# Attention and gated MLP on one core: batches 0 and 1 read q and k as six tokens per partition with both heads side by side, the strided scores of the other batches take 36 rows, and the three lists of steps are written anew

## The chip, the cores and the metric

The kernel runs on one core of a Trainium2 chip. A core has five engines that run side by side and each take their own instructions in order: TensorE (PE; its weight loads are shown apart as PEld), VectorE (DVE), ScalarE (ACT), GpSimd (POOL) and SyncE (SP), which here only issues transfers. Sixteen DMA engines move data between HBM and the core's memory, SBUF; TensorE writes to PSUM, which this kernel uses as four slots of two banks. The metric is device time in microseconds (us); lower is better.

## The reference, cut to what matters

Eight batches, eight heads, 576 positions, head size 64, all float32. Heads 0 to 3 have a local mask (a window of 32), heads 4 to 7 a strided mask (every 32nd position). The attention's output is the input of a gated MLP that mixes positions with a 576x576 matrix.

```python
scores = scale * np.matmul(q, k.transpose(0, 1, 3, 2))
mask_local = (rel >= 0) & (rel < stride)
mask_strided = (rel >= 0) & (pos[None, :] % stride == pos[:, None] % stride)
masks = np.stack([mask_local if h < H // 2 else mask_strided for h in range(H)], axis=0)
scores = np.where(masks[None, :, :, :], scores, -1000000000.0)
...
attn = attn / (np.sum(attn, axis=-1, keepdims=True) + 1e-09)
return np.matmul(attn, v).astype(np.float32)
...
h = x @ w_in                      # then gelu, split in u and v
v_n = (v - mu) / np.sqrt(var + 1e-06) * g_ln
v_s = np.einsum('ts,bsd->btd', w_sg, v_n) + b_sg[None, :, None]
gated = u * v_s
return (x + gated @ w_out).astype(np.float32)
```

## The kernel before, in words

Two heads share the 128 partitions: a pair is called hh (0 and 1 local, 2 and 3 strided). Per batch, the attention of four pairs gives x, and the MLP runs on it in four stages of matmuls: `v` and `u` (x times the two halves of w_in), `sg` (the mixing of positions) and `o` (w_out). Float32 factors are split in a high and a low part of a type that TensorE takes in one pass, so each product is three matmuls (names ending in h and l: `wih`, `wil`, `wsh`, `wsl`, `woh`, `wol`; `xt`, `vg` hold both parts). In the first batch's stretch all weights are loaded and split too, by ACT, DVE and POOL.

Nothing is scheduled by a program while the kernel is built: each engine gets its instructions in the order in which the steps stand in three lists of words. `START` is run once (batch 0's attention, the weights, batch 0's MLP beside batch 1's attention), `CYCLE` for batches 1 to 6 (the MLP of batch b, the attention of b + 1, loads for b + 2), `LAST` for batch 7. In a word like `SB^:0` the letters name the step (the table `STEPS`), the number is its pair or chunk, `@2` the PSUM slots it takes, `^` that the step's other engine does it (DVE in place of POOL, ACT in place of DVE, DVE in place of ACT or POOL in place of DVE, by the step). A sign behind the letters says which batch is meant: `-` the current one, none the next one for capital letters, `+` the one after; `=` marks steps of the weights.

The steps of this change: `LR` (`row_load`), `RQ` and `RK` (`row_turn`), `CQ` and `CK` (`row_copy`) bring q and k of batches 0 and 1 to SBUF and turn them so that the head's 64 numbers lie along the partitions. Before, a partition gets nine tokens of one head, 2304 bytes in one piece, and a turn is 18 plain float32 matmuls of 64x64 against the identity, which TensorE runs in two passes (36 records). Batches 2 to 7 take another way: `LQ` (`qk_load`) and `TQ` (`qk_transpose`, on DVE), which is kept. `SS` (`strided_scores`) makes 32 small matmuls per pair, `MK` (`sm_mask`) adds the mask on DVE, `MX`, `SB`, `EX`, `SU`, `ML` are the other steps of the softmax, `PS` and `PL` turn the weights of attention on TensorE, `PV`, `PW`, `VA` multiply them with v. `XH`, `XL`, `XR`, `XD` split x, transpose it and store it to HBM (from the ACT queue) for the residual.

Profile rows name the outputs: `tqq`, `tqk` (turns), `sa`, `sr` (local scores), `ss` (strided scores), `ptl`, `pts` (turned weights of attention), `ol`, `os` (their products with v). In the order's rows a name carries a running number.

Of the kernel before, what the change touches and what calls it, by code (L numbers as in the profile page):

```python
# [31 lines left out]
ch=:3 SB-:3 VY-@0:0 CL-:4 VX-:0 cd=:9 MX-:2 XH-:1 EX-:3 SB-:2 ch=:0 cc=:4 cl=:13 XR-:0 XHa-:0
XL-:1 RQ@3:1 RK@2:1 XHb-:0 cg=:9 XR-:1 EX-:2 LV-:2 ca=:6 SU-:2 CK:1 XLb-:0 RK@3:0 TZ:0 SU-:3 cb=:6
ch=:9 ML-:2 CQ:1 ML-^:3 XD-:0 XD-:1 PS-@1:2 RQ@2:0 LV-:3 CS-:2 cb=:2 PS-@0:3 cb=:8 CK:0 XLa-:0
cc=:6 CS-:3 cc=:2 wb= PV-@1:2 CQ^:0 PW-:2 cd=:4 cc=:8 XH-:2 wc= cl=:5 SL@2:0 cd=:6 PV-@3:3 cd=:2
wl=:0 SL@0:1 wd= cl=:7 XL-:2 cg=:2 we= LR:2 cg=:4 ch=:2 ca=:13 LZ:0 lg= PW-:3 XR-:2 MK:0 va@1:0
cd=^:8 ch=^:4 XH-:3 vb:0 ca=:5 wl=:4 cb=:5 XD-:2 cb=:13 ca=:7 wt=@2:0 vc:0 cl=:11 LR:3 XL-:3 cc=:5
wh=:0 cg=:8 vd:0 RQ@0:2 xt RK@2:2 g:0 cb=:7 CQ:2 MX:0 v@1:2 va@0:1 vb:1 CK:2 ca=:11 wm=:0 wo=
cd=^:5 cc=:7 wl=:2 cg=:6 ls:0 vc:1 lm:0 ch=:8 cd=:7 vh vl LV:0 cb=:11 SB^:0 cc=:11 cg=:5 cl=:10
wp= cg=:7 LQ+:0 lr:0 wt=@2:4 ch=:5 cc=:13 vd:1 LZ:1 EX:0 ch=:7 ch=^:6 XR-:3 g:1 SU:0 cd=^:13  # L40
RK@3:3 RQ@1:3 CK:3 cg=:13 CQ^:3 u@3:2 SS@1:2 u@0:1 wh=:4 cd=:11 lh:0 LV:1 g:2 wt=@1:2 u@3:0 ca=:10
ls:1 TZ+:0 ug:2 cl=:15 ll:0 MK:2 ug:1 cb=:10 XD-:3 SS@2:3 u@3:3 wh=:2 lm:1 ls:2 cg=:11 lr:1 wm=:4
ML:0 cc=:10 wl=:3 lr:2 ch=:11 ug:0 lm:2 lh:1 wt=@1:3 ca=:15 ug:3 lh:2 MX:2 MK:3 wm=:2 cb=:15
cd=:10 wh=:3 MX:3 ll:1 ll:2 wm=:3 cl=:14 TQ+:0 SB:3 cc=:15 SB:2 EX:2 cg=:10 TZ+:1 LQ+:1 cd=^:15
SU:2 PL@23:0 cl=:12 s@0:0 CL:0 s@1:1 sm:0 CM:0 VA@3:1 EX:3 ML:2 TQ+:1 sh:0 PS@1:2 VA@2:0 sm:1
ca=:12 s@0:2 XR:1 cb=:12 cg=:15 cc=:12 ch=:15 ch=:10 sh:1 ch=:13 s@1:3 SU:3 LQ+:3 CS:2 ca=:14 XH:1
sl^:0 sm:2 XL:1 XH:0 sl^:1 XD:1 cd=^:12 LV:2 LV:3 o@3:2 XL:0 cg=:12 cb=:14 ML:3 PV@2:2 XR:0 rt
cc=:14 sh:2 XD:0 sm:3 ch=:12 PW:2 PS@1:3 sl^:2 o@0:0 cd=^:14 sh:3 LZ+:1 o:1 XH:2 CS:3 r sl:3 o:3
PV@1:3 PW:3 XR:2 cg=:14 ch=^:14 LV+:1 o2:0 XR:3 LQ+:2 XH:3 XD:3 XL:2 o2:1 LZ+:0 os:1 o2:3 os:0
# [7 lines left out]
CM^:0 sh:2 SU:2 sm:3 sl^:2 o@0:0 VA@2:1 TQ+:0 sh:3 LV:2 VA@1:0 o@3:4 o:1 sl^:3 EX:3 XH:0 XH:1 ML:2
SU:3 o2:1 XR:0 LV:3 XL:0 o2:4 os:1 o@1:2 o2:0 os:4 TQ+:1 od:1 os:0 o2:2 ML^:3 LZ+:0 os:2 PS@0:2
od:4 PS@3:3 XR:1 XD:0 od:0 XL:1 o:3 CS:3 o2:3 CS:2 XD:1 PV@2:3 LQ+:2 od:2 PV@3:2 PW:3 PW:2 XH:2
os:3 LZ+:1 XH:3 XR:2 XL:3 XR:3 LV+:1 XD:3 XL:2 XD:2 od:3 LV+:0  # L60
# [980 lines left out]
```

## Time and profile before

| | us |
|---|---|
| median of three runs | 577.9 (572.86 to 579.85) |
| the profiled execution, its own time | 579.74 |
| its span, first to last instruction | 577.9 |
| PE busy in the span | 550.6 (95%) |
| DVE busy in the span | 377.2 (65%) |
| ACT, POOL busy in the span | 205.7 (36%), 187.7 (32%) |

The page of the profile tells how long each engine was busy, then cuts the span into 40 slices of 14.4 us with the busy share of each in tenths. The views of the trace used below are stretches of time (busy us of each engine, DMA share and rate), waits (what ended an engine's idle time), the timeline of one engine (instructions of one form merged, with the idle time ahead of them in brackets) and groups of instructions by form (busy us, mean ns of one). Where instructions overlap, as matmuls do, the time that one costs is the distance from its start to the next one's, not its length.

### The profile page before, as it was taken

How to read it: one execution, taken by the hardware profiler on the slowest of the kernel's cores; microseconds unless marked ns; L12 is line 12 of the kernel's file. 1: busy time of each engine (PE TensorE's matmuls, PEld its weight loads, DVE VectorE, ACT ScalarE, POOL GpSimd, SP SyncE). 2: the span in 40 equal slices, each digit the busy share in tenths (PEclk: the TensorE clock that was granted, in tenths of full speed). 3: DMA queues.
4: the chain of work that ended last, by engine and by line, in shares of the span. 5: the costliest groups of instructions: out<-in, count | busy, mean ns of one | idle time of the engine just before them, and what ended most of it. 6: DMA issues, size and time to landing. Idle time of an engine off the chain costs nothing.

```text
span 577.9 us, 17955 instructions
## 1 busy us (share of the span) xinstructions
PE 550.6 (95%) x7699; PEld 494.6 (86%) x7699; DVE 377.2 (65%) x685; ACT 205.7 (36%) x330; POOL 187.7 (32%) x407
## 2 busy tenths in 40 slices
PE   6777998999999899999999999999999999999997
...
GB/s 303 238 171 195 113 154 117 165 203 164 38 1 164 158 197 29 11 185 168 163 1 84 199 205 59 2 179 196 151 1 89 195 180 1 1 140 140 2 1 91
DMA packets 244593, 70.13 MB, mean 121 GB/s; under 512 B 228193, under 2 KB 228193, under 8 KB 244514
## 3 DMA queue, kind: packets, MB, share of 16 engines
...
q8 instruction: 60, 0.98, 0.7%
...
## 4 chain that ended last, share of the span: by engine, by line
PE 85%; DMA 7%; DVE 4%; issue 2%; ACT 1%; SPq 1%; ACTq 0%; DVEq 0%
PE sg L82 21%; PE v L82 19%; PE u L82 17%; PE o L82 14%; DMA out_dram<-ob 3%; PE ss L82 3%; PE ol L82 3%; PE os L82 3%; PE sa L82 2%; DMA xd<-xs 1%; DMA stage<-in_moe_w_in_dram 1%; PE ptl L82 1%; DVE ob L82 1%; PE tqq L82 1%; PE pts L82 1%
## 5 line engine op out<-in xcount | busy, mean ns | idle before, releaser
L82 PE MATMUL sg<-wsh,vg 128*128 128x288 f32 x512 | 114.1, 298 | 0.0
L82 PE MATMUL u<-xt,wih 128*128 128x288 f32 x512 | 103.2, 297 | 1.0 <-ACT u L82 1.0
L82 PE MATMUL o<-woh,vg 128*128 128x512 f32 x288 | 94.1, 396 | 2.2 <-DVE ob L82 2.2
L82 PE MATMUL v<-wih,xt 128*128 128x512 f32 x256 | 85.5, 405 | 2.1 <-DVE xs L82 2.1
L82 PEld LDWEIGHTS sg<-wsh,vg 128*128 128x128 f32 x512 | 86.6, 190 | 0.0
L82 PEld LDWEIGHTS u<-xt,wih 128*128 128x128 f32 x512 | 82.2, 188 | 2.1 <-ACT u L82 1.2
L82 PE MATMUL sg<-wsl,vg 128*128 128x288 f32 x256 | 76.1, 297 | 0.1
L82 PE MATMUL u<-xt,wil 128*128 128x288 f32 x256 | 75.5, 295 | 0.0
L82 PEld LDWEIGHTS o<-woh,vg 128*128 128x128 f32 x288 | 54.1, 188 | 13.9 <-DVE ob L82 2.8
L82 DVE TENSOR_TENSOR gt<-sg,u 128x576 f32<-128x576 f32 x32 | 24.2, 757 | 56.6 <-PE sg L82 35.7
L82 PEld LDWEIGHTS v<-wih,xt 128*128 128x128 f32 x256 | 49.1, 192 | 11.4
L82 PE MATMUL o<-wol,vg 128*128 128x512 f32 x144 | 56.3, 391 | 0.0
L82 POOL TENSOR_TENSOR vg<-gt,vg 128x576 fp32r<-128x576 f32 (+2 forms) x45 | 44.8, 1016 | 34.8 <-ACT vg L82 34.8
L82 PE MATMUL v<-wil,xt 128*128 128x512 f32 x128 | 50.9, 398 | 0.0
L82 PEld LDWEIGHTS sg<-wsl,vg 128*128 128x128 f32 x256 | 48.8, 191 | 0.3 <-DVE wsl L82 0.3
L82 DVE TENSOR_TENSOR ob<-o,xn 128x512 f32<-128x512 f32 x32 | 22.0, 691 | 41.3 <-PE o L82 32.8
L82 PEld LDWEIGHTS u<-xt,wil 128*128 128x128 f32 x256 | 48.1, 188 | 0.0
L82 ACT ACT_TABLE_LOAD x18 | 23.1, 1283 | 59.5 <-DMA xd<-xs 58.6
L82 ACT CAST vg<-gt 128x576 fp32r<-128x576 f32 (+2 forms) x48 | 23.1, 514 | 58.1 <-DVE gt L82 53.8
L82 DVE BATCH_NORM_STATS2 bnst<-hv 128x6 f32<-128x512 f32 (+1 forms) x40 | 27.1, 677 | 24.2 <-ACT hv L82 23.9
L82 ACT ACTIVATE u<-u 128x576 f32<-128x576 f32 x32 | 20.0, 649 | 57.0 <-PE u L82 56.5
L82 POOL TENSOR_TENSOR sml<-sml,sr 128x1152 f32<-128x1152 f32 (+2 forms) x9 | 17.2, 1906 | 68.6 <-DVE sr L82 62.7
...
## 6 DMA issues: line engine op xcount, KB each, us to landing
xd<-xs ACTq DMA_DIRECT2D x128, 72.0 KB
...
```

Source lines behind the costliest of these rows:

```text
L82: ins = self.tc.keep_in_program_order(op(*args, **kwargs))
```

## The change

Four edits in the code, and new lists.

A partition now gets six tokens with both heads side by side, so 96 partitions hold a pair. A head's part of a partition is six pieces of 64 numbers, 256 bytes each, and each tensor of a pair is loaded by two DMAs in place of one. The turn is six transposes of 96x128 in place of 18 matmuls of 64x64; the copy from PSUM rearranges accordingly.

For batches 2 to 7 the strided scores take 36 columns of q in place of 64, so that the mask is added in two pieces of 36 partitions, as it was for batches 0 and 1 before, and the memset behind q's last column goes away. A helper tile of `v_tail_copy` is half as long.

```diff
-    ROWS = S // 9
+    ROWS = S // 6
...
         if b == 0:
-            both = p1.tile([P, 2, 9 * D], F32, tag=HOMES[hh], name=f"rows_{b}_{hh}")
+            both = p1.tile([P, 2, 6, P], F32, tag=HOMES[hh], name=f"rows_{b}_{hh}")
...
-            sp.dma_start(
-                raw, src[b, 2 * hh : 2 * hh + 2].rearrange("h (p j) d -> (h p) (j d)", j=9)
+            for hp in range(2):
+                sp.dma_start(
+                    raw[:, :, D * hp : D * hp + D],
+                    src[b, 2 * hh + hp].rearrange("(p j) d -> p j d", j=6),
+                )
...
+        for j in range(6):
+            pe.transpose(
+                ps[:, j // 3, j % 3 * ROWS : j % 3 * ROWS + ROWS], raw[:, j], ident[0:ROWS, 0:ROWS]
             )
...
-        for j in range(9):
-            for hp in range(2):
-                r = slice(ROWS * hp, ROWS * hp + ROWS)
-                pe.matmul(
-                    ps[64 * hp : 64 * hp + 64, j * ROWS : j * ROWS + ROWS],
-                    raw[r, j * D : j * D + D], ident[r, r],
-                    start=True, stop=True,
-                )
...
-                if nm == "q":
-                    pool.memset(tt[:, S : S + ST], 0.0)
...
-                            rows, qc, kc = 64, slice(c * TP, c * TP + 64), slice(c * TP, c * TP + TP)
+                            qc = slice(c * TP, c * TP + TP)
...
-            for r in (slice(0, TP), slice(64, 100)) if b < 2 else (slice(0, 100),):
-                n = r.stop - r.start
+            for r in (slice(0, TP), slice(64, 64 + TP)):
...
-LR-:0 LR-:1 RQ-@2:0 cl=:3 mk= TZ-:0 TZ-:1 RK-@3:0 CQ-^:0 ml= mp=@2 cl=:1 cl=:0 ca=:3 cb=:3 LR-:3
+LR-:0 cl=:3 cl=:1 TZ-:0 RQ-@2:0 LR-:1 RK-@3:0 mk= ca=:1 ca=:3 mp=@1 cl=:0 CK-:0 cb=:1 cb=:3
...
-ug:0 rt lh:1 ll:0 lr:2 u@3:2 ll:1 lh:2 ll:2 MK:3 SB:2 ug:2 SB^:0 s@1:1 sm:1 MX:3 ug:3 EX:2 s@0:0
+lm:2 MK:2 lh:2 ll:0 EX:0 MK:3 ll:1 u@2:3 MX:2 ll:2 SU:0 u@1:0 TZ+:1 s@0:1 TZ+:0 sm:1 TQ+:1 SB^:2
```

What the lists move is seen where the instructions stand. SP's first transfers before: `rows` are q and k of batch 0, `stage` a part of w_in, `cs` of w_out, `wsg` of the mixing matrix, `v` the values.

```order
L82 DMA rows_0_92<-in_q_dram 128x576
L82 DMA rows_0_92<-in_k_dram 128x576
L82 DMA rows_1_95<-in_q_dram 128x576
L82 DMA rows_1_95<-in_k_dram 128x576
L82 DMA stage<-in_moe_w_in_dram 128x1024 x3
L82 DMA rows_3_192<-in_q_dram 128x576
L82 DMA rows_3_192<-in_k_dram 128x576
```

And now, from the same place on, as far as the values of the first two pairs:

```order
L82 DMA rows_0_92<-in_q_dram 96x6x64 x2
L82 DMA rows_0_92<-in_k_dram 96x6x64 x2
L82 DMA stage<-in_moe_w_in_dram 128x1024 x2
L82 DMA rows_1_108<-in_q_dram 96x6x64 x2
L82 DMA rows_1_108<-in_k_dram 96x6x64 x2
L82 DMA stage<-in_moe_w_in_dram 128x1024
L82 DMA rows_3_165<-in_q_dram 96x6x64 x2
L82 DMA rows_3_165<-in_k_dram 96x6x64 x2
L82 DMA rows_2_209<-in_q_dram 96x6x64 x2
L82 DMA rows_2_209<-in_k_dram 96x6x64 x2
```

The loads of the rows have moved little against each other; each is now two DMAs of short pieces. The values of pair 0 come ahead of those of pair 1, and batch 1's first rows (`rowsq_1`, `rowsk_1`) stand between the two.

TensorE in the same stretch, the turns of batch 1 and the first products with the values, before:

```order
L82 MATMUL ol_1_568<-ptl_5_563,v_1_398 64x32 x36
L82 MATMUL ol_0_616<-ptl_5_563,v_0_396 64x32 x4
L82 MATMUL ol_0_616<-ptl_4_621,v_0_396 64x32 x32
L82 MATMUL tqq_1_669<-ident,rowsq_1_504 64x64 x18
L82 MATMUL tqk_1_688<-ident,rowsk_1_506 64x64 x18
L82 MATMUL tqk_0_724<-ident,rowsk_0_612 64x64 x18
L82 MATMUL pts_2_765<-ident,sms_89 128x100 x8
```

and now:

```order
L82 MATMUL ol_0_495<-ptl_5_482,v_0_248 64x32 x4
L82 MATMUL ol_0_495<-ptl_4_493,v_0_248 64x32 x32
L82 MATMUL tqk_1_538<-ident,rowsk_1_397 128x96 x6
L82 MATMUL ol_1_567<-ptl_5_482,v_1_252 64x32 x36
L82 MATMUL pts_2_623<-ident,sms_89 128x100 x8
L82 MATMUL tqq_0_635<-ident,rowsq_0_476 128x96 x6
L82 MATMUL tqq_1_649<-ident,rowsq_1_394 128x96 x6
```

Turns have gone from 18 rows to 6 each, and a turn of batch 1 now stands between the products of pair 0 and pair 1.

ACT in one round of `CYCLE` (batch 2), between the last parts of the normalised v (`t`) and the first gated product (`gt`), before; `sml` and `sms` are the exponentials of the local and the strided scores, and ACT_TABLE_LOAD changes between the tables of gelu and of the exponential:

```order
L82 ACTIVATE t_85<-hv_2_3210,y_2_3383 64x512
L82 ACTIVATE u_2_3431<-u_2_3399 128x576
L82 ACTIVATE u_3_3467<-u_3_3296 128x576
L82 ACT_TABLE_LOAD
L82 ACTIVATE sms_89<-sms_89 100x16x36
L82 ACTIVATE sml_3108<-sml_3108 128x1152
L82 CAST vg<-gt_1_3463 128x576
```

and now:

```order
L82 ACTIVATE t_85<-hv_2_2977,y_2_3181 64x512
L82 ACT_TABLE_LOAD
L82 ACTIVATE sml_2932<-sml_2932 128x1152
L82 ACT_TABLE_LOAD
L82 ACTIVATE u_3_3307<-u_3_3211 128x576
L82 ACTIVATE u_0_3309<-u_0_3243 128x576
L82 CAST vg<-gt_1_3301 128x576
L82 ACT_TABLE_LOAD
L82 ACTIVATE sms_89<-sms_89 100x16x36
```

The local exponential has moved ahead of the last two gelus, so that each round has four table loads in place of two; the whole program has 30 in place of 18. In `CYCLE` TensorE's stages keep their order (v, u, sg, o); the two strided scores stand together in the middle of u (before: one inside v, one after the first quarter of u), and v's first half stands ahead of the local scores.

## Rows read from the trace of the kernel before

**Rows 1.** The page: busy time and share of PE and DVE, and PE's busy tenths in 40 slices.

```profile
PE 550.6 (95%) x7699; PEld 494.6 (86%) x7699; DVE 377.2 (65%) x685; ACT 205.7 (36%) x330; POOL 187.7 (32%) x407
...
PE   6777998999999899999999999999999999999997
```

**Rows 2.** Stretches of the span: from:to, length, then busy us (and instructions) of PE, PEld, DVE, ACT, POOL, the granted share of PE's clock, the DMA share, GB/s. The first is what stands ahead of the first v matmul, the second the rest of batch 0's way to sg, the last a round of CYCLE.

```profile
0.00:50.00 50.00, 33.59 (x1152) 30.74 (x1152) 35.66 (x69) 23.73 (x43) 19.14 (x45) 0.96 0.86 245
50.00:90.00 40.00, 38.96 (x467) 34.42 (x462) 32.63 (x60) 25.07 (x43) 26.67 (x54) 0.96 0.64 131
...
125.00:195.00 70.00, 67.65 (x969) 60.46 (x968) 45.90 (x82) 21.91 (x35) 19.50 (x47) 1.00 0.52 109
```

**Rows 3.** Who PE waited for, us in total, times, longest; the first 95 us.

```profile
PE tqq L82 <- issue: 4.7, 2, 2.9
PE tqq L82 <- DMA rows<-in_q_dram: 4.0, 1, 4.0
PE sr L82 <- issue: 2.9, 1, 2.9
PE sg L82 <- DVE t L82: 1.5, 1, 1.5
...
PE u L82 <- ACT u L82: 1.0, 1, 1.0
```

**Rows 4.** The same from 95 us to the end of the span, the two largest (a third, of 0.2 us, is left).

```profile
PE o L82 <- DVE ob L82: 2.2, 3, 1.2
PE v L82 <- DVE xs L82: 2.1, 1, 2.1
```

**Rows 5.** PE's timeline: start, length, instructions merged, and in brackets the idle time ahead with what ended it. The first two turns, the three stalls that end in "issue", the first v matmuls, two turns between v matmuls, and the first chunk of u with what follows it.

```profile
3.99 2.19 PE L82 MATMUL tqq<-ident,rows 64*64 64x64 f32 x36 [3.99 <-DMA rows<-in_q_dram]
5.94 2.16 PE L82 MATMUL tqk<-ident,rows 64*64 64x64 f32 x36
...
20.61 0.62 PE L82 MATMUL tqq<-ident,rows 64*64 64x64 f32 x13 [2.92 <-issue]
...
33.67 0.97 PE L82 MATMUL tqq<-ident,rowsq 64*64 64x64 f32 x26 [1.82 <-issue]
...
42.37 1.14 PE L82 MATMUL os<-pts,v 36*64 36x36 f32 x64 [1.22 <-ACT pts L82]
...
48.95 0.42 PE L82 MATMUL sr<-kT,qT 64*32 64x64 f32 x10 [2.89 <-issue]
...
50.10 0.79 PE L82 MATMUL v<-wih,xt 128*128 128x512 f32 x1
...
57.70 1.26 PE L82 MATMUL tqq<-ident,rowsq 64*64 64x64 f32 x36
58.80 1.22 PE L82 MATMUL tqk<-ident,rowsk 64*64 64x64 f32 x36
...
70.34 0.54 PE L82 MATMUL u<-xt,wih 128*128 128x288 f32 x2
...
73.72 1.30 PE L82 MATMUL ss<-kT,qT 64*36 64x36 f32 x64
```

**Rows 6.** PE's timeline: eight transposes of 100x128 in the first stretch and what follows them, and sixteen in a round of CYCLE and what follows.

```profile
38.21 0.91 PE L82 MATMUL pts<-ident,sms 100*128 100x100 f32 x8
39.05 1.26 PE L82 MATMUL tqq<-ident,rowsq 64*64 64x64 f32 x36
...
185.46 1.56 PE L82 MATMUL pts<-ident,sms 100*128 100x100 f32 x16 [0.22 <-DVE ob L82]
186.80 0.47 PE L82 MATMUL o<-woh,vg 128*128 128x512 f32 x1
```

**Rows 7.** The page's list of DMA queues: PE's instructions come in the queue named q8 (kind: packets, MB, share of 16 engines).

```profile
q8 instruction: 60, 0.98, 0.7%
```

**Rows 8.** Stretches with the columns of rows 2. From 2 to 6 us the rows of 2304 bytes are on their way; from 20 to 24 mostly pieces of 256 bytes of the values; from 30 to 42 the last transfers ahead of the first v matmul.

```profile
2.00:6.00 4.00, 2.01 (x38) 2.04 (x40) 0.00 (x0) 0.20 (x1) 3.46 (x18) 1.00 0.96 305
...
20.00:22.00 2.00, 1.35 (x22) 1.02 (x22) 1.80 (x5) 0.73 (x2) 0.00 (x0) 1.00 0.94 129
22.00:24.00 2.00, 2.00 (x81) 2.00 (x83) 1.35 (x4) 1.96 (x6) 1.05 (x1) 0.57 1.11 187
...
30.00:36.00 6.00, 3.92 (x172) 3.64 (x164) 5.54 (x12) 3.60 (x8) 3.73 (x5) 1.00 0.56 190
36.00:42.00 6.00, 4.13 (x88) 3.69 (x88) 5.93 (x13) 1.28 (x3) 1.52 (x2) 1.00 0.74 139
```

**Rows 9.** SP's timeline: the issue of the values of pairs 0 and 1 (pieces of 256 bytes) and of pairs 2 and 3.

```profile
13.74 10.61 SPq L82 DMA_DIRECT2D v<-in_v_dram  x8
...
31.68 6.81 SPq L82 DMA_DIRECT2D v<-in_v_dram  x4
```

**Rows 10.** Groups by form, whole span: busy us, mean ns of one. Strided scores with 64 and with 36 columns of q on PE, the mask on DVE in one piece and in two, the table loads of ACT.

```profile
L82 PE MATMUL ss<-kT,qT 64*64 64x36 f32 x768 | 13.7, 224 | 0.0
L82 PE MATMUL ss<-kT,qT 64*36 64x36 f32 x256 | 5.3, 248 | 0.1
L82 DVE TENSOR_TENSOR sms<-ss,mask_s 100x576 f32<-100x576 f32 x12 | 9.0, 748 | 0.2
L82 DVE TENSOR_TENSOR sms<-ss,mask_s 36x576 f32<-36x576 f32 x8 | 6.0, 754 | 3.0 <-PE ss L82 3.0
L82 ACT ACT_TABLE_LOAD x18 | 23.1, 1283 | 59.5 <-DMA xd<-xs 58.6 <-PEq L1023 0.7
```

More of the change, by code (lines that the diff above doesn't have):

```diff
@@ L32 @@
[L32 to L49, printed above, removed]
@@ new lines @@
+SS-@1:2 LV-:1 wh=:1 MK-:2 ca=:4 PL-@30:5 wm=:1 TZ:0 LR:0 CL-:5 cc=:9 SB-:3 PL-@1:4 MX-:2 CL-:4
+VY-@2:0 SB-:2 cd=^:9 CM-:5 cg=:0 VX-:0 cg=:9 RK@3:1 cc=:2 ch=^:9 EX-:3 XR-:0 cb=:4 ca=:8 cb=:8
+TZ:1 EX-:2 SU-:2 CK:1 SU-:3 cc=:8 VA-@0:1 cc=:4 cl=:6 ML-:2 XD-:0 XH-:1 XHa-:0 ML-:3 XR-:1 LV-:2
+LV-:3 PS-@1:2 cl=:5 CS-:2 RQ@3:0 XHb-:0 cd=:8 XL-:1 ca=:6 wb= RQ@1:1 PS-@0:3 PV-@1:2 XLb-:0 wc=
+cb=:6 cl=:13 CQ:0 XD-:1 CS-:3 LR:2 LZ:1 CQ^:1 PW-:2 RK@2:0 PV-@3:3 ch=^:0 XLa-:0 XH-:2 cd=:2 cc=:6
+CK:0 XL-:2 PW-:3 wl=:0 cd=^:4 cl=:7 wd= cg=:8 XH-:3 we= SL@2:0 SL@0:1 va@1:0 XR-:2 vb:0 cg=:4
@@ new lines @@
+cg=:2 XL-:3 ch=:2 ca=:13 wt=@2:0 ca=:5 vc:0 xt wo= XD-:2 vd:0 RQ@2:2 MK:0 ch=^:4 RK@0:2 wh=:0
+cb=:5 g:0 cb=:13 wp= MX:0 cd=:6 CQ:2 v@1:2 va@2:1 cl=:11 lg= LR:3 wm=:0 vb:1 LV:1 cc=:5 wl=:4
+RQ@0:3 ca=:11 ca=:7 LQ+:1 cd=^:5 cg=:6 cg=:5 vh CK:2 ls:0 vc:1 cb=:11 cb=:7 LZ:0 cc=:11 vd:1
+RK@3:3 cc=:13 cc=:7 SB^:0 EX:0 XR-:3 wl=:2 cd=^:7 lr:0 cl=:15 g:1 SS@1:2 vl cg=:7 CQ^:3 ch=^:5
+wt=@0:4 SU:0 g:2 ch=^:7 XD-:3 lm:0 cd=:13 cl=:10 ls:1 cd=^:11 ch=:6 MK:2 CK:3 u@2:1 lm:1 wl=:3
+wh=:4 u@3:2 ML:0 lh:0 wt=@1:2 lr:1 LV:0 ls:2 ug:1 ug:2 SS@2:3 wh=:2 u@3:3 lh:1 LQ+:0 cl=:12 ug:3
@@ new lines @@
+lm:2 LV:3 wt=@2:3 MK:3 u@0:0 lr:2 ll:0 ca=:10 ca=:15 cg=:13 wm=:4 MX:2 wh=:3 lh:2 LQ+:3 ll:1 wm=:2
+wm=:3 ch=:8 TZ+:1 PL@12:0 ll:2 CL:0 cb=:15 cl=:14 cb=:10 cc=:15 ug:0 SB^:2 MX:3 CM:0 s@3:0 TQ+:1
+SB^:3 cd=^:15 cg=:11 cc=:10 sm:0 EX:2 cd=^:10 cg=:10 cg=:15 sh:0 SU:2 EX:3 ch=:13 s@0:1 ca=:12
+sm:1 VA@3:1 XH:1 ML:2 TZ+:0 VA@2:0 TQ+:0 SU:3 PS@1:2 CS:2 XR:1 ML^:3 ch=^:11 XH:0 XD:1 sh:1 sl^:0
+ch=:10 ca=:14 s@0:2 PS@1:3 XL:1 cb=:12 LV:2 s@3:3 rt cc=:12 sl^:1 sm:2 CS^:3 sm:3 o@0:0 sh:2
+cd=:12 r sl^:2 XR:0 cb=:14 XL:0 o@3:2 ch=^:15 o:1 PV@2:3 sh:3 cc=:14 PV@1:2 sl^:3 cg=:12 LZ+:0
@@ L57 @@
[L57 to L60, printed above, removed]
+LQ+:0 v1@0:0 SL@2:0 SL@1:1 v2:0 g:0 MK:0 xt v@2:2 v1@1:1 v2:1 TQ:2 MX:0 vh ls:0 u@2:1 SB:0 g:1 vl
+u@0:2 lr:0 SS@1:2 g:2 lm:0 ug:1 ls:1 lh:0 r lm:1 ug:2 rt lr:1 TQ:3 SS@3:3 ls:2 LQ+:1 lr:2 lh:1
@@ new lines @@
+lm:2 MK:2 lh:2 ll:0 EX:0 MK:3 ll:1 u@2:3 MX:2 ll:2 SU:0 u@1:0 TZ+:1 s@0:1 TZ+:0 sm:1 TQ+:1 SB^:2
+ug:3 ug:0 s@3:0 ML:0 PL@20:0 MX:3 sm:0 sh:1 EX:2 sh:0 SB:3 SU:2 sl^:1 s@1:2 s@3:3 sm:2 TQ+:0 LV:3
+sh:2 CL:0 CM^:0 sm:3 sh:3 VA@0:0 sl:3 sl^:0 VA@3:1 EX:3 o@1:0 XH:0 sl^:2 o:1 o@2:4 XH:1 SU:3 o2:1
+LQ+:2 ML^:3 XR:0 XL:0 o2:4 os:1 o@0:2 o2:0 o2:2 od:1 XL:1 os:4 ML:2 os:0 od:4 LV:2 XD:0 LZ+:0
+PS@1:3 XR:1 od:0 PS@3:2 os:2 CS:2 o:3 o2:3 CS^:3 LZ+:1 PV@1:2 PV@2:3 PW:2 os:3 XD:1 LQ+:3 PW:3
+LV+:1 XH:3 od:3 XH:2 XR:3 od:2 XL:3 XD:3 XL:2 XR:2 XD:2 LV+:0
@@ L67 @@
+s@3:0 s@2:2 sm:0 sh:1 sh:0 sm:3 sm:2 sl^:1 sh:3 sl:3 sh:2 sl^:0 o@0:2 o:3 sl:2 o2:3 o@1:0 os:3
+od:3 o2:2 o2:0 os:2 o@2:4 os:0 o2:4 od:2 os:4 od:0 od:4 o:1 o2:1 os:1 od:1
 """
```

47 lines of the change are left out of this document (20 added, 27 removed).

## The prediction, made before the changed kernel was run

> **What bounds the kernel now.** I read the page first: PE is busy 95% of the span, DVE 65%, and the slices show where PE is not: in the first five, and almost nowhere else [rows 1]. The stretches say it in numbers: PE is idle for 16.4 of the first 50 us, for 1.0 of the next 40, and for 2.4 of a round of CYCLE [rows 2]. So there are two kernels here. From about 50 us on PE sets the pace, and only shorter PE work or a removed wait counts. Ahead of that PE waits, and the question is for what. The list of waits answers in part [rows 3]: 4.0 us for the first rows, which nothing can hide, 7.6 us in three stalls that end in "issue", that is for nothing the profile shows, and 1.0 to 1.5 us here and there for DVE or ACT. Behind 95 us all PE waits together are 4.5 us [rows 4]; that is the most that new lists can win in CYCLE and LAST.
>
> I take the three stalls for late instructions. They stand at 20.6, 33.7 and 48.9 us [rows 5], where PE runs many tiny matmuls. PE's 15,398 instructions (7,699 matmuls and as many weight loads) [rows 1] come in 60 packets of 16 KB [rows 7], so some 257 each, and a turn alone is 72 of them. The stalls come in the stretch whose DMA share is 0.56 to 1.11 [rows 8], so a packet can be late there. The Trainium skill (Runtime: NRT & Kernel Launch, Instruction fetch mechanics) says that engines fetch blocks of 256 instructions ahead and that this is mostly hidden. The packet count agrees; the hiding doesn't, if my reading is right, and by the page's rule the stalls would have another cause and could stay, which is 7.6 us less to win in the fast rival below.
>
> **The turns.** A turn between v matmuls takes 1.10 us at the full clock (57.70 to 58.80), and the first one, at the low level, 1.95 [rows 5]. The new one is six transposes of 96x128. The nearest rows are those of 100x128: eight take 0.84 us, sixteen take 1.34 [rows 6], so 84 to 105 ns each and 0.50 to 0.63 us per turn. No row shows one at the low clock; twice that, 1.0 to 1.26, is the bound. I take 0.55 and a saving of 0.55. Twelve of the sixteen turns stand ahead of the first v matmul (6.6 us of PE work), four behind it (2.2 us). They also take 16 x 60 = 960 instructions out of PE's stream, which is 3.7 of 60 packets, most of them where the stalls are. PE therefore could reach v 6.6 + 7.6 = 14 us earlier, if its operands were there.
>
> **The loads speak against it.** A pair's q and k are 2 x 294,912 bytes. In pieces of 2304 bytes such rows came at 305 GB/s (2 to 6 us, DMA share 0.96): 1.9 us. In pieces of 256 bytes, from 20 to 24 us, the values came at 129 to 187 GB/s with a DMA share of 0.94 to 1.11 [rows 8]: 3.2 to 4.6 us per pair. So each pair costs 1.2 to 2.7 us more of all sixteen engines, and six pairs are needed ahead of v: 7 to 16 us. The Trainium skill (DMA: Bandwidth & Descriptors, Why small descriptors are slow) gives 3 cycles of overhead to the 8 of a 256-byte descriptor; by that alone, as an estimate, a pair would cost about a third more, 0.6 us, and six 4 us. The trace shows more, and I go by its rows.
>
> Is there room? Until 24 us the DMA share is about 1, so there is none; from 30 to 42 us it is 0.56 and 0.74 [rows 8], which leaves 6 x 0.44 + 6 x 0.26 = 4.2 us. The last loads needed ahead of v are the values of pairs 2 and 3, issued from 31.68 to 38.5 [rows 9] and used at 42.37 and after; PE then waits for ACT, not for them [rows 5]. They would come 7 - 4 = 3 to 16 - 4 = 12 us later. I put their landing before at about 40 to 41 (two to three us behind the last issue, an estimate), so 43 to 53 now, and behind it are one product with the values and the local scores of batch 1, which PE does in about 3.5 us. First v matmul: 47 to 56, against 50.1 now. DVE does 35.7 us of work in these 50 [rows 2], of which the new lists change little, so from its first work on it could not let v start before about 41 to 42 either. Within 47 to 56 I take 49.5, nearer to the low end, because PE work no longer adds to it and the values of pair 0 now come ahead of pair 1's: a gain of 0.6 us. That is the core of the forecast: the turns get shorter, and the time goes to the transfers.
>
> **Behind the first v matmul.** Four turns save 2.2 us of PE work that is on the path, since PE was idle for only 1.0 of 40 us there [rows 2]. The waits for `u` (1.0) and `t` (1.5) [rows 3] stay or go with DVE and ACT; DVE has 32.6 us of work in 40 [rows 2], so it has room. I take 1.0 of 2.5.
>
> **Edits that I cost at nothing.** Strided scores of 36 columns: the same number of matmuls. The 64-column form takes 13.7/12 = 1.14 us per pair, the 36-column one 5.3/4 = 1.32 [rows 10], but the latter has strided columns of q, which the new one has not. Bounds 0 to +2.2 us (12 x 0.18); I take 0. The mask: two pieces of 754 ns for one of 748 [rows 10], 12 x 0.76 = 9.1 us more on DVE, 1.5 per round; DVE is busy 45.9 of 70 us there [rows 2]. Queued behind it are the low parts of the normalised v, which sg waits for; without cover it would cost the 1.5 us per round, 9 us in all. Two chunks of u stand between the strided scores and sg, 2 x 3.4 = 6.8 us (70.34 to 73.72 is one) [rows 5]; in that time DVE has two masks of 1.5, two low parts of two operations each and two short steps, some 6 to 7 us: just covered. The twelve more table loads: 12 x 1.283 = 15.4 us of ACT [rows 10], 2.6 per round; ACT is busy 21.9 of 70 us. They delay the last two gelus of u, which are next needed when the second of four sg products is done; ACT has 48 us free per round to catch up. Memsets taken off POOL hide in its idle time.
>
> **CYCLE and LAST.** PE's stages keep their order, and it waits 4.5 us in all [rows 4]. New lists could take these waits away or set up new ones. I count 1.5 us gained, with bounds from -4.5 to +6 (one us more in each of six rounds).
>
> **The sum.** -0.6 (ahead of v) - 2.2 - 1.0 (behind) - 1.5 (rounds) = -5.3 us. The profiled execution's own time is 579.7, so 574.4; that execution stands 1.8 us above the median of 577.9, and against the median it is 572.6, say 573.
>
> **The rivals.**
>
> *The transfers don't bind (fast).* If short pieces cost the low end (7 us) and the room takes 4.2 of them, PE reaches v when DVE allows, at about 42 to 43, 7.5 us earlier. With 3.2 behind and 2 in the rounds that is 577.9 - 12.7 = 565. For it: most of the loads were early before, PE's only long wait for rows is the 4.0 us at the start [rows 3]. Against it: the DMA share near 1 until 24 us, and the stalls may have another cause.
>
> *The transfers bind hard (slower).* At 129 GB/s the loads come 12 us late, the first v matmul moves to 55.5, and PE, idle by stretches, starts it at the low level, where a turn took 1.95 us in place of 1.10 [rows 5]; I allow 1 us for that. +5.4 + 1 - 2.2 = +4, 582. It is slower than before from the point where six pairs cost over some 12 us more, that is at a rate below about 150 GB/s.
>
> *A wait in each round (slower or same).* If DVE's second mask isn't covered, the low parts come 1 to 1.5 us late in six rounds: 573 + 6 to 9 + 1.5 = 580 to 583. DVE has 24 us free per round [rows 2], but the stretch does not tell where.
>
> *The change doesn't do what it says.* Transposes at the low clock as dear as the matmuls were, and the stalls stay: no term of the turns, loads late by 3 us: 578.
>
> **Chances.** Forecast 0.47, fast 0.23, hard 0.15, a wait in each round 0.10, no effect 0.05. Faster by over 2% is below 566.3: most of the fast case and a little of the forecast, 0.20. Slower by over 2% is above 589.5: only where the hard case and the wait in each round come together or are worse than their rows, 0.08. Same: 0.72 (2% is about what a measurement of this kernel can tell from no change). Range: from 562, the fast case with three more us in the rounds, to 585, the hard case and its error; the forecast's own is 568 to 578.
>
> **What would show it.** Turns: six transposes in 0.5 to 0.65 us between v matmuls; more would break that term. Stalls: PE waits ending in "issue" ahead of v should fall from 7.6 us to under 3, and 56 or 57 packets in PE's instruction queue. Loads: PE waits named by rows or values should appear in the first 45 us, with a DMA share near 1 up to about 40 us; if there are none, the fast rival holds. The first v matmul at 47 to 52. Rounds: PE busy at least 68 of 70 us and no DVE wait ahead of sg; if DVE waits of over 1 us stand there in each round, the third rival holds. A first v matmul before 44, or rounds that change by over 1 us each, would make the forecast wrong.

## The result, and the profile after

| | before | after |
|---|---|---|
| median of 20 runs, us | 577.7 (571.5 to 583.0) | 583.8 (578.0 to 590.3) |
| profiled execution: own time, span, us | 579.7, 577.9 | 581.3, 579.2 |
| first v matmul starts at, us | 50.1 | 55.1 |
| last `os` of batch 1 ends at, us | 119.8 | 118.4 |
| from there to the last matmul, us | 454.4 | 457.2 |

The change made the kernel slower: ratio 1.0107, 95% interval 1.0073 to 1.0142. 573 was forecast; the time lies inside the range, on the other side of no change. Ratios here and below leave out runs in the chip's slower state, which the medians keep, so a ratio and its medians can differ by some 0.3%. The profiled execution of after lies 2.5 us under its median and that of before 2.0 above, so the pair shows 1.6 of the 6.1 us. Another profile of after is among the experiments.

The page of after, for [rows 1] and [rows 7]; the fourth line is PE's granted clock in slices:

```profile
PE 543.1 (94%) x7219; PEld 486.7 (84%) x7219; DVE 395.2 (68%) x641; ACT 219.7 (38%) x337; POOL 205.1 (35%) x456
...
PE   3769999999999899999999999999999999999997
...
PEclk9965999999999999999999999999999999999999
...
q8 instruction: 56, 0.92, 0.7%
```

PE has 7.5 us less work and the kernel takes longer. DVE, POOL and ACT have 18, 17 and 14 us more. Stretches of after, for [rows 2] and [rows 8] (columns as there):

```profile
0.00:50.00 50.00, 32.21 (x628) 28.17 (x628) 31.29 (x59) 22.63 (x42) 19.07 (x45) 0.84 1.03 215
50.00:90.00 40.00, 37.57 (x492) 32.88 (x489) 35.41 (x60) 25.41 (x46) 21.52 (x46) 0.91 0.88 168
125.00:195.00 70.00, 69.53 (x1025) 62.27 (x1027) 49.66 (x74) 24.92 (x37) 23.59 (x58) 1.00 0.57 120
...
36.00:42.00 6.00, 3.84 (x80) 3.52 (x80) 5.22 (x11) 1.72 (x3) 2.36 (x2) 0.50 1.05 220
```

The DMA share is 1.03 over the first 50 us (0.86 before), and from 36 to 42 us PE stands at the low level, 1.2 GHz (granted 0.50; the trace has it there from 33.7 to 57.6). The waits of PE up to 95 us, for [rows 3]:

```profile
PE tqq L82 <- DMA rows<-in_q_dram: 9.0, 2, 4.8
PE ol L82 <- DMA v<-in_v_dram: 2.2, 2, 1.7
PE tqk L82 <- DMA rows<-in_k_dram: 1.7, 2, 1.1
PE tqk L82 <- DMA rowsk<-in_k_dram: 1.4, 1, 1.4
```

And from 95 us on, for [rows 4]:

```profile
PE sg L82 <- DVE t L82: 3.9, 5, 1.0
PE u L82 <- DVE hv L82: 1.9, 3, 1.0
PE ptl L82 <- POOL sml L82: 1.8, 5, 0.4
PE ol L82 <- issue: 1.6, 2, 0.9
PE v L82 <- issue: 1.6, 1, 1.6
```

Ahead of v the "issue" stalls are gone (7.6 us to 1.2) and waits for rows and values stand in their place. From 95 us on the waits have grown from 4.5 us to 12.1. PE's timeline of two turns between v matmuls, for [rows 5]:

```profile
62.39 0.66 PE L82 MATMUL tqq<-ident,rowsq 96*128 96x96 f32 x6
62.89 0.66 PE L82 MATMUL tqk<-ident,rowsk 96*128 96x96 f32 x6
```

And the groups by form, for [rows 10]:

```profile
L82 ACT ACT_TABLE_LOAD x30 | 38.5, 1283 | 58.2 <-DMA xd<-xs 27.1 <-DMA v<-in_v_dram 20.3 <-issue 9.7
L82 DVE TENSOR_TENSOR sms<-ss,mask_s 36x576 f32<-36x576 f32 x32 | 24.1, 754 | 2.0 <-PE ss L82 1.6
L82 PE MATMUL ss<-kT,qT 64*36 64x36 f32 x1024 | 13.7, 213 | 0.7 <-ACT qT L82 0.7
```

A turn takes 0.50 us (start to start). The 36-column scores take 13.7 us for all sixteen pairs; before it was 13.7 for the twelve of 64 columns and 5.3 for the four of 36.

### The profile page after: what moved, and what is told of

Its sections match the earlier page's. It is cut to its first block, busy times and chain, and to the rows that moved or that the text cites. A ratio compares the mean times of both kernels' runs of the same rounds, so it can differ in the third digit from the quotient of the medians.

```text
span 579.2 us, 16986 instructions
## 1 busy us (share of the span) xinstructions
PE 543.1 (94%) x7219; PEld 486.7 (84%) x7219; DVE 395.2 (68%) x641; ACT 219.7 (38%) x337; POOL 205.1 (35%) x456
## 4 chain that ended last, share of the span: by engine, by line
PE 44%; POOL 13%; DMA 10%; DVE 10%; SPq 9%; ACT 7%; issue 6%; ACTq 1%; DVEq 0%
PE o L82 15%; PE sg L82 10%; SPq L82 9%; POOL nt L82 6%; PE v L82 6%; DMA xd<-xs 4%; DMA v<-in_v_dram 4%; PE ol L82 3%; PE u L82 3%; POOL y L82 3%; PE os L82 2%; ACT L82 2%; POOL va L82 2%; DVE bnst L82 2%; POOL sml L82 2%
## 5 line engine op out<-in xcount | busy, mean ns | idle before, releaser
L82 PE MATMUL sg<-wsh,vg 128*128 128x288 f32 x512 | 112.9, 296 | 0.0
L82 PE MATMUL o<-woh,vg 128*128 128x512 f32 x288 | 92.8, 395 | 0.7 <-DVE gt L82 0.7
L82 POOL TENSOR_TENSOR vg<-gt,vg 128x576 fp32r<-128x576 f32 (+2 forms) x35 | 36.0, 1053 | 30.9 <-ACT vg L82 30.9
L82 POOL MEMSET v<- 32x128 f32 x16 | 2.9, 198 | 95.0 <-PE os L82 54.4
L82 ACT ACTIVATE vg<-hv,y 128x512 fp32r<-128x512 f32 x32 | 21.4, 716 | 31.6 <-POOL y L82 24.3
```

Of the source, the lines that this page charges most:

```text
L82: ins = self.tc.keep_in_program_order(op(*args, **kwargs))
```

## The experiments

The theories: **A**, the 256-byte loads cost; **B**, the new lists of the rounds cost; **C**, the second mask piece costs. After the first four runs a fourth came up, **D**: where PE's packets of 256 instructions end. Ratios are to the kernel before on the same chip; e10 and e15 to e18 follow in the text.

| run | START | rounds, LAST | rows, scores | tiny matmuls | median us | ratio (95%) |
|---|---|---|---|---|---|---|
| e1 | old | old | new, new | 0 | 595.8 | 1.0304 (1.0250 to 1.0359) |
| e2 | new | new | old, old | 0 | 604.6 | 1.0481 (1.0414 to 1.0547) |
| e3 | old | new | new, new | 0 | 585.0 | 1.0120 (1.0064 to 1.0175) |
| e4 | new | old | new, new | 0 | 590.9 | 1.0237 (1.0182 to 1.0292) |
| e5 | old | old | new, new | 80 | 576.8 | 0.9989 (0.9954 to 1.0023) |
| e6 | old | old | old, new | 0 | 573.8 | 0.9946 (0.9906 to 0.9986) |
| e7 | old | old | new, old | 0 | 596.8 | 1.0317 (1.0257 to 1.0377) |
| e8 | new | new | new, new | 96 | 581.0 | 1.0062 (1.0028 to 1.0095) |
| e9 | old | old | long pieces, new | 48 | 581.4 | 1.0024 (0.9987 to 1.0061) |
| e11 | new | old | new, new | 80 | 572.5 | 0.9917 (0.9884 to 0.9949) |
| e12 | old | old | old, old | 48 | 597.3 | 1.0314 (1.0266 to 1.0362) |
| e13 | new | new | new, new | 80 | 580.8 | 1.0057 (1.0026 to 1.0088) |
| e14 | new | old | old, new | 0 | 579.1 | 1.0007 (0.9968 to 1.0046) |

**Swapping the parts (e1 to e4).** The edits put lists or functions of one kernel into the other, as

```diff
 # e4, in the kernel after
-LQ+:0 v1@0:0 SL@2:0 SL@1:1 v2:0 g:0 MK:0 xt v@2:2 v1@1:1 v2:1 TQ:2 MX:0 vh ls:0 u@2:1 SB:0 g:1 vl
+SL@0:0 v1@1:0 r SL@2:1 TQ:3 v2:0 TQ:2 MK:0 g:0 v1@3:1 xt v2:1 ls:0 SS@1:2 lm:0 LQ+:0 g:1 v@2:2
...
```

e1: 

> The new rows, turns, copies, 36-row scores and masks under the three old lists. Theory B (the rounds lose by the new order of the cycle, the scores themselves gain about 0.84 us in each of six rounds): 573 to 575 us. Theory A (the 256-byte loads ahead of the first v matmul are the whole loss, whatever the lists): 582 to 585, with the first v matmul near 55 and TensorE waiting over 8 us for the tiles rows and v. Theory C (the mask in two pieces loads DVE and delays the rounds): 582 or more, with waits for DVE in the rounds and the first v matmul near 50.

e2: 

> The old rows in nine-token pieces, old turns, old 64-row scores and one-piece mask, under the three new lists. Theory B: slower than the kernel after, since the waits of the new rounds (about 7.6 us more than before) stay and the 0.8 us per round of the shorter scores is gone: 584 to 588. Theory A: with long pieces the start is as before, 577 to 579.

e3: 

> The kernel after with the first list alone put back. Theory A (the loads' size is the loss): no change, 583 to 585. If the new order of the first list is the loss: 577 to 579. Theory B: 583 to 585, with the waits in the rounds as in the kernel after (sg, u and ptl for DVE and POOL, 7 us or more).

e4: 

> The kernel after with the lists of the rounds and of the last batch put back, the new first list kept. Theory B: the waits in the rounds fall to under 5 us and the shorter scores gain: 576 to 579, about 6 us below the kernel after. Theory A: no change, 583 to 585.

No mixture came near an expectation except e3: all four were slower than before, three of them slower than after. e3 has the waits of after's rounds again (from 95 us on 3.5 us of `sg` for `t`, 2.5 of `u` for `hv`, 1.4 of `ptl` for `sml`). For the others the largest wait of PE says why, in e1 over the whole span (e4 has 11.3 us, six times):

```profile
PE sa L82 <- issue: 11.2, 6, 2.1
```

And in e2:

```profile
PE ss L82 <- POOL qT L82: 17.9, 6, 3.4
```

In e2 the new order meets the memset on POOL that the change removed, in every round: without that edit, which I costed at nothing, PE waits 17.9 us in the new order. In e1 PE stops at `sa` once in START and in five of the six rounds, waiting for nothing that the list of waits shows. Two of these places in e1's timeline:

```profile
195.85 2.07 PE L82 MATMUL os<-pts,v 36*64 36x36 f32 x128
197.85 0.65 PE L82 MATMUL sa<-kT,qT 64*32 64x64 f32 x38
200.59 0.84 PE L82 MATMUL sa<-kT,qT 64*32 64x64 f32 x34 [2.10 <-issue]
...
267.87 0.70 PE L82 MATMUL sa<-kT,qT 64*32 64x64 f32 x24 [1.94 <-issue]
```

And two stretches from one stall to the next:

```profile
200.59:267.87 67.28, 65.34 (x892) 58.42 (x893) 46.40 (x82) 21.54 (x31) 18.59 (x40) 0.96 0.59 113
267.87:336.63 68.76, 66.84 (x893) 59.74 (x893) 46.97 (x83) 21.90 (x35) 19.15 (x44) 0.97 0.59 115
```

From stall to stall there are 1,785 and 1,786 matmuls and weight loads of PE (892 + 893, 893 + 893). With PE's semaphore instructions, which the trace has and the views leave out, it is 1,792 each time: seven packets of 256. The rounds themselves have 1,771 and 1,795 such instructions in turn, so a packet ends at nearly the same place in each: behind 38, 48, 47, 57 and 56 of the 72 `sa` records. Just ahead PE goes through 128 `os` matmuls with their weight loads, 256 instructions, in 2.00 us. That is theory D: a packet consumed that fast ends before the next is there. (The 4 us in the text of e5 below are an estimate: these 2.0 and the 2.1 of the stall.)

The traces can say it directly, since they hold the transfers of PE's packets (queue q8) too. In e1 a packet is on its way from 197.98 to 199.20 us, and PE, idle from 198.50, goes on at 200.59. In all twenty traces PE has 72 waits of over 0.5 us that end in "issue", those ahead of v in the kernel before among them. 71 of them end 1.2 to 1.9 us behind the landing of a packet, and when PE's instructions are counted from its first record, these 71 stand at counts that are all whole packets of 256 apart. Of the 277 other waits of that length 7 stand at such a count.

**The packets' ends (e5, e7, e12, e8).** e5 adds to e1, and e12 to the kernel before, only this (e8 adds 96 in the same way to the kernel after; e7 is the kernel before with the new rows and the halved tile of `v_tail_copy`):

```diff
-            pe.matmul(ps[:, 0, 0 : 2 * P], bits[:, 0:P], bits, start=True, stop=True)
+            pe.matmul(ps[0:16, 0, 0:16], bits[:, 0:16], bits[:, 0:16], start=True, stop=True)
 START, e5:
-RK-@3:0
+hw=:30 RK-@3:0
...
-RK-@1:2
+hw=:50 RK-@1:2
 START, e12:
-RK-@3:0
+hw=:24 RK-@3:0
...
-RK-@1:2
+hw=:24 RK-@1:2
```

Their results are discarded. e5: 

> The new code under the old lists again, with 80 tiny matmuls (16 columns, discarded) put ahead of two turns of the first list that wait anyway. Theory D: TensorE runs out of instructions where two ends of its 256-instruction packets stand under 4 us apart; a round has 1792 instructions, 7 packets, so the stall (2 us, six times at sa in the run of the new code under the old lists, 11.2 us, each followed by half clock) returns at one place in every round, and which place is set by the count of instructions in the first list. The 160 instructions move the ends to places at least 6 us apart: the six issue waits at sa disappear, and 577 to 582 us. If the stalls have another cause (the order of the rounds itself): no change, 593 to 598.

e7: 

> The kernel before with the six-token rows, their loads, turns and copies alone. Theory D: 962 instructions fewer in the first list put the packets' ends in the rounds at sa as in the new code under the old lists: six issue waits at sa of about 2 us, 596 to 602. Theory A (the loads alone cost): no such waits, first v matmul near 55 and 580 to 584.

e12: 

> The kernel before, with nothing but 48 tiny matmuls (96 instructions, 16 columns, discarded) ahead of two turns of the first list. Theory D: they move the packets' ends in its rounds to sa, 1.8 us after the last one: issue waits of about 2 us at sa in most rounds, with half clock behind them, and 590 to 597. Rival (the place of the ends matters only for the new code): 577 to 580.

e8: 

> The kernel after with 96 tiny matmuls (192 instructions) ahead of two waiting turns of the first list. Theory D: the packets' ends in its rounds come to stand at least 4.5 us apart; the issue waits at v and ol (1.6, 1.1 and 0.9 us in the profiled run) go: 579 to 582. Theory B: its other waits (sg, u, ptl for DVE and POOL) stay as they are, 7 to 9 us, so that it doesn't come under 577.

Theory D holds each time. 80 useless matmuls take e1 from 595.8 to 576.8; 48 of them take the kernel before from 578.2 on that chip to 597.3, so it is not their own work that counts; the six-token rows alone (e7), 480 matmuls fewer, cost 19 us, with the same stall. PE's largest wait from 123 us on, in e7:

```profile
PE sa L82 <- issue: 9.4, 5, 2.3
```

in e12:

```profile
PE sa L82 <- issue: 9.6, 5, 2.3
```

and in e5, which has no "issue" wait there at all:

```profile
PE u L82 <- DVE hv L82: 1.9, 3, 1.1
```

Each stall costs more than itself. In e1, the stretch ahead of one, the one with it, and the next:

```profile
190.00:198.50 8.50, 8.45 (x201) 6.91 (x199) 3.98 (x6) 1.69 (x3) 0.39 (x2) 1.00 1.07 208
198.50:206.50 8.00, 5.91 (x46) 4.40 (x46) 5.07 (x6) 0.67 (x2) 0.61 (x1) 0.57 0.88 147
206.50:213.00 6.50, 6.50 (x97) 5.49 (x97) 4.83 (x8) 2.31 (x2) 0.00 (x0) 1.00 0.94 220
```

Behind this stall PE runs mostly at the low level (granted 0.57). From the end of `os` of batch 1 to the last matmul e1 takes 462.7 us and e5 447.8: 14.9 us, of which 9.4 are the stalls. The kernel after has such stalls too, smaller (1.6 at v, 1.6 at ol above); shifting them away gives 2.8 us (e8), though the intervals overlap.

**The scores and masks alone (e6).** 

> The kernel before with the 36-row scores, the two-piece mask and without the memset alone; the count of instructions on TensorE and so the places of the packets' ends are those of the kernel before. Theory D with the gain of 0.84 us per round from the shorter scores: 571 to 574. Theory C (the second mask piece on DVE delays the rounds): 578 to 586, with waits for DVE ahead of the transposes of the scores.

```diff
-                            rows, qc, kc = TP, slice(c, S, NCL), slice(c, S, NCL)
+                            qc = slice(c, S, NCL)
...
-            for r in (slice(0, TP), slice(64, 100)) if b < 2 else (slice(0, 100),):
+            for r in (slice(0, TP), slice(64, 64 + TP)):
```

573.8 us, as D expected. PE's largest waits behind 119 us are 1.7 for `xt` and 0.8 for instructions, none for the mask. Theory C falls, under the old order of the rounds. What was gained is in PE's timeline. The 64 columns of a pair before, and the first v matmul behind them:

```profile
138.86 1.14 PE L82 MATMUL ss<-kT,qT 64*64 64x36 f32 x64
139.93 0.50 PE L82 MATMUL v<-wih,xtl 128*128 128x512 f32 x1
```

and the same place in e6:

```profile
137.97 0.79 PE L82 MATMUL ss<-kT,qT 64*36 64x36 f32 x64
138.69 0.50 PE L82 MATMUL v<-wih,xtl 128*128 128x512 f32 x1
```

A pair takes 0.72 us from start to start in place of 1.07. The pairs of batches 0 and 1, whose 36 columns are strided, still take 1.31 (74.27 to 75.58 in e6), also at the full clock.

**The loads (e9, e14).** e9 takes e5's kernel with one transfer per tensor:

```diff
-            for hp in range(2):
-                sp.dma_start(
-                    raw[:, :, D * hp : D * hp + D],
-                    src[b, 2 * hh + hp].rearrange("(p j) d -> p j d", j=6),
-                )
+            raw = raw.rearrange("p a b -> p (a b)").rearrange("p (h x) -> p h x", h=2)
+            sp.dma_start(raw, src[b, 2 * hh : 2 * hh + 2].rearrange("h (p j) d -> p h (j d)", j=6))
...
+            for hp in range(2):
+                pe.matmul(
+                    ps[D * hp : D * hp + D, j // 3, j % 3 * ROWS : j % 3 * ROWS + ROWS],
+                    raw[:, hp, j * D : j * D + D], ident[0:ROWS, 0:ROWS],
```

> The new code under the old lists, but each tensor of six-token rows loaded by one transfer in pieces of 1536 bytes (head after head on the free axis), and turned by twelve plain matmuls of 64 columns; 48 tiny matmuls ahead of two turns keep the packets' ends out of sa. Theory A (the 256-byte pieces are what the new rows cost): 573 to 575, like the kernel before with the new scores alone (573.8), with under 6 us of waits for the tiles rows. If the cost lies in the turns or copies of six tokens: 576 to 578, as with short pieces.

e14: 

> Old nine-token rows in long pieces, 36-row scores, the new first list, the old rounds. If the six-token rows with 256-byte pieces cost under any list: 568 to 571, below the 572.5 of six-token rows under the same lists, and the waits for the tiles rows (9.3 us there) fall under 4. Rival (under the new first list the 36 instruction pairs of an old turn cost more than the loads give back): 574 to 579, with issue waits at turns.

In e9 PE's waits for rows fell as theory A says, but others came, and the time missed both expectations. PE's waits for rows in e5 up to 95 us:

```profile
PE tqk L82 <- DMA rowsk<-in_k_dram: 4.5, 2, 2.8
PE tqk L82 <- DMA rows<-in_k_dram: 3.8, 2, 2.4
```

And three of e9's, whole span:

```profile
PE ol L82 <- issue: 5.5, 1, 5.5
PE ss L82 <- issue: 2.8, 2, 2.5
PE tqk L82 <- DMA rows<-in_k_dram: 0.7, 1, 0.7
```

The turns of e9 are 24 instruction pairs, not 6, the first v matmul comes at 61.9 (55.8 in e5), and the time is no better. The 5.5 us are a late packet too: it is on its way from 37.87 to 38.91, and PE goes on at 40.51. Why it set out only 2.9 us after PE had stopped stays open. In e14 the rival held: PE waits 5.3 us for instructions ahead of v (2.0 at `sa`, 1.3, 1.1 and 0.9 at three others); in e11 no such wait of 1 us is left. Under the old START the six-token rows cost 0.43% (e5 against e6), which is within the error; under the new one they are 0.9% faster than nine-token rows (e11 against e14), which have those 5.3 us of stalls. So the size of the pieces can't be given a price of its own here: each list was made for one layout.

**The rounds' lists (e11, e13).** Both have the same START with 80 tiny matmuls; only the rounds' lists differ.

e11: 

> The kernel after with the lists of the rounds and the last batch put back, and 80 tiny matmuls (160 instructions) in the first list. Theory D: the stalls at sa of the same kernel without them (11.3 us of waits, 590.9 us in all) disappear; theory B: without the waits of the new rounds the rest comes to 575 to 578. If it stays above 580, the new first list is what costs.

e13: 

> The kernel after with the same 80 tiny matmuls at the same places as in the run of it with the old rounds (572.5 us): the instructions of the first list and their packets are then the same, and only the lists of the rounds and the last batch differ. Theory B (the new rounds' lists lose by waits for DVE and GpSimd): 577 to 581, with 4 us or more of waits for t, sml and ob that the other run hasn't, and a longer stretch from the end of os of the second batch to the end. Rival (the difference came from the first list's packets): 571 to 575.

572.5 against 580.8: theory B, 1.4% or 8.1 us. e11 is faster than it was expected to be, and faster than both kernels of this case. From the end of `os` of batch 1 to the last matmul, e11 (columns of [rows 2]):

```profile
115.41:564.21 448.80, 445.92 (x5677) 399.73 (x5676) 301.24 (x539) 145.45 (x223) 131.99 (x286) 1.00 0.52 108
```

The same of e13:

```profile
119.52:576.59 457.07, 445.26 (x5677) 399.75 (x5676) 305.17 (x480) 159.55 (x229) 154.76 (x351) 1.00 0.51 106
```

And PE's waits in e13 behind 116 us:

```profile
PE u L82 <- DVE hv L82: 2.9, 3, 1.9
PE sg L82 <- DVE t L82: 2.7, 4, 0.9
PE ptl L82 <- POOL sml L82: 1.8, 5, 0.4
PE o L82 <- DVE ob L82: 1.4, 1, 1.4
PE pts L82 <- DVE ob L82: 1.2, 1, 1.2
```

PE has the same work and takes 8.3 us longer; all its waits there come to 11.6 us, against 2.9 in e11, where no cause has more than 0.9. (The profiles differ by 4.1 us ahead of that too, where the lists are the same: e13's lies 1.5 us above its median, e11's 2.8 below.) Other traces agree: the same stretch takes 446.3 to 449.0 us wherever the old rounds run with the new scores and without stalls at `sa` (e5, e6, e9, e11, e14), and 451.7 to 458.1 with the new rounds (after, e3, e8, e13, e15). Four moves within the new list (`lr` makes the root of a chunk, `lh` and `ll` its high and low part, `vl` is the addition in the last tokens of v):

```diff
 # e10 (with 96 tiny matmuls), e16
-rt lr:1 TQ:3 SS@3:3 ls:2 LQ+:1
+rt lr^:1 TQ:3 SS@3:3 ls:2 LQ+:1
+rt TQ:3 SS@3:3 ls:2 lr^:1 LQ+:1
 # e17
-vh ls:0 u@2:1 SB:0 g:1 vl
+vh vl ls:0 u@2:1 SB:0 g:1
 # e18
-MK:2 lh:2 ll:0 EX:0 MK:3
+MK:2 EX:0 lh:2 ll:0 MK:3
```

e10: 

> The kernel after, shifted as before, and in the rounds' list the reciprocal root of chunk 1 sent back from GpSimd to DVE. Theory B (three of these chains in series on GpSimd make lh:2, ll:2 and so sg and ptl late): the waits of sg for DVE (t) and of ptl for GpSimd (sml) go, 577 to 579. Rival (another part of the new rounds' list costs): 580 to 582.

e16: 

> The kernel after with 80 tiny matmuls, and the reciprocal root of chunk 1 on DVE, now behind the transposes of k and the statistics of chunk 2 (in front of the transposes it made ss wait six times 1.9 us). Theory B: the waits of sg for t and of ptl for sml go, 2 to 4 us below the same kernel without it. Rival (these waits have another cause in the new order, or DVE only hands them on): within 1 us of it or slower.

e17: 

> The kernel after with 80 tiny matmuls, and in the rounds' list the addition for the last 64 tokens of v moved from behind the statistics of chunk 0 and the subtraction on GpSimd to in front of them (DVE then takes it as soon as ScalarE's copy is there). If the five kinds of wait in the new rounds are separate and each costs its own: the waits of u for hv (2.9 us) go and the time is 577 to 579. Rival (a wait in these rounds is handed on, as when the root went to DVE): 580 to 584, with more of the waits for t or sml.

e18: 

> The kernel after with 80 tiny matmuls, and in the rounds' list the exponential of the local scores one place earlier on ScalarE, ahead of lh:2, which waits 3.65 us for GpSimd there. In the run without it DVE stands 2.3 us before the sums of this exponential, and with them what DVE does next and the product on GpSimd that ptl waits for. Theory (the new rounds lose by this chain from the exponential over DVE to GpSimd): DVE's wait for ScalarE (sml, 12.8 us in six rounds) and the waits of ptl for sml (1.8 us) go, and 576 to 579. Rival (only handed on, as with the root and the addition): 580 to 584, with the waits of sg for t and of u for hv unchanged or longer.

e10 took 591.0 us (ratio 1.0223), e16 585.1 (1.0133, 1.0087 to 1.0180), e17 582.3 (1.0074, 1.0041 to 1.0108), e18 578.5 (1.0047, 1.0014 to 1.0079), beside 580.8 (1.0057) without a move. PE's largest waits behind 123 us, e10:

```profile
PE ss L82 <- DVE kT L82: 11.1, 6, 1.9
```

e16:

```profile
PE sg L82 <- DVE t L82: 4.8, 6, 0.8
PE u L82 <- DVE sms L82: 4.6, 6, 0.9
```

e17 (in e18 the same line has 3.1 us, 3 times):

```profile
PE sg L82 <- DVE t L82: 5.5, 5, 1.3
```

With the root on DVE, what stood behind it is late: the transposes of k in e10, the low part `t` and the masks in e16. With `vl` ahead in e17, `t`. Only e18 took a wait away without setting up a larger one: e13's DVE stood for `lh:2` and then for the exponential, and in e18 the second of these is gone. DVE's timeline in e13:

```profile
223.51 0.75 DVE L82 SCALAR_TENSOR_TENSOR t<-hv,y,t 64x512 fp32r<-64x512 f32 x1 [1.51 <-ACT t L82]
226.60 1.35 DVE L82 TENSOR_REDUCE sr<-sml 128x18 f32<-128x1152 f32 x1 [2.34 <-ACT sml L82]
```

And in e18:

```profile
221.65 0.74 DVE L82 SCALAR_TENSOR_TENSOR t<-hv,y,t 64x512 fp32r<-64x512 f32 x1 [1.77 <-ACT t L82]
222.43 1.35 DVE L82 TENSOR_REDUCE sr<-sml 128x18 f32<-128x1152 f32 x1
```

PE's waits of `ptl` for `sml` went with it, as expected. The median fell by 2.3 us, but by the ratios it is 0.6 and the intervals of e13 and e18 overlap, so its worth lies between nothing and some 2 us.

**After, once more (e15).** 

> The kernel after, unchanged, profiled once more, since its first profile lay 2.5 us under its median: theory B and D expect the waits of the first profile for t, hv, sml and for instructions at v and ol again, more of them in total if this run is nearer the median of 583.8 us.

 It took 582.0 us; from the end of `os` of batch 1 to the last matmul 458.1, and the same waits: `u` for `hv` 2.9, `sg` for `t` 2.1, `ptl` for `sml` 1.4, `ol` and `v` for instructions 1.8 and 1.1. In total it is 10.3 us from 95 us on, less than the first profile's 12.1, so the expected growth didn't come. The end of the second batch's `os` stands at 118.3, as in the first profile: the loss lies behind it.

## Why the prediction was wrong, point by point

A chain from before to after, each step the difference of two ratios (about 0.5% of error each, so that the new rounds' lists and the new START are clear of it, the scores and the packets' ends barely, the rows not): scores -0.54% (e6); six-token rows under the old START +0.43% (e5); new START -0.72% (e11); new rounds' lists +1.40% (e13); the packets' ends of after itself +0.50%. Together +1.07%, 6.2 us. That the time lies inside the range is luck: 585 was there for late loads, and the loss came in the rounds.

- **The step that failed: CYCLE and LAST, "I count 1.5 us gained, with bounds from -4.5 to +6".** They cost 8.1 us with START and its packets equal, outside the bounds. That PE waited 4.5 us behind 95 us was right, and so that little could be won there; what I had not asked was what stands ahead of each low part on DVE, and of `lh:2` on POOL, in the new order. That the new order of CYCLE costs is shown (e11 against e13); which of its moves makes how much of the 8.1 us stays open. LAST has no share: from the last `os` of the round before it to the last matmul it takes 54.2 us in e11 and e13 alike (510.0 to 564.2, 522.4 to 576.6).
- **"A wait in each round" was a rival with 0.10, at 580 to 583.** Place and size were right (8.1 us for its 6 to 9), the cause half: the mask alone is free (e6), but the new list puts TQ:3 and MK:3 on DVE between the statistics and `ll:2`, some 2.2 and 1.5 us in e13, where the old one has TQ:3 well ahead and MK:3 behind. That this is why the moves to DVE fail is argued from the lists and was not tried. The rival's sign came weaker than it was named: `sg` waits for `t` five times, 1.0 us at most, and the one round of the forecast's sign, 125 to 195, has PE busy for 69.5 of 70 us.
- **Scores, costed at 0 with bounds 0 to +2.2.** They gained 3.1 us. The nearest row of 36 columns had strided operands; the new form of the rounds has plain slices of q and k, and takes 0.72 us where 64 columns took 1.07 and 36 strided ones 1.31 (e6): 12 x 0.35 = 4.2 us less. Fewer columns were the term, not the count of matmuls.
- **Turns, 0.55 us.** 0.50 at the full clock; where 0.50 was granted, 0.98 (two turns from 42.18 to 44.13) to 1.15 (47.74 to 48.89): right. One reading ahead of it was not: no row shows the old first turn, 1.95 us, at the low level, since [rows 8] has 1.00 for 2 to 6 us. Stalls and packets: "issue" ahead of v from 7.6 to 1.2 us, 56 packets: right, and the reading of the three stalls as late instructions too (they end 1.2 to 1.9 us behind a packet's landing).
- **The loads.** The first v matmul came at 55.1, not 49.5, with the DMA share above 1 and PE at the low level: the hard rival's picture and its 55.5. But its price didn't follow. The stretch from the first v matmul to the end of `os` of batch 1 took 63.3 us and not 69.7, with 60.9 us of PE work in place of 67.1; its waits are 2.3 us, as good as before (2.5). The shorter turns are some 2.4 us of that (4 x 0.6); six matmuls of `o`, some 1.4 us, only moved behind this `os`; the granted clock was 0.98 and not 0.95. So the second batch's `os` ended 1.4 us earlier than before, and with the moved work the two kernels are level there. What comes late ahead of v is not lost when the work behind it shrinks by as much.
- **A mechanism that no step had.** I counted 960 instructions fewer as a gain ahead of v only. They also move the ends of all later packets, which is worth up to 3.2% (e7 and e12 against before).
